# A fused attention, expert and GLU kernel: the second head's moves ahead of later loads, fills and RMS weights later, RMS in smaller steps

## The chip, the cores and the metric

The kernel runs on one core of a Trainium2 chip. Its time is the device time of one execution in microseconds (us). Before the change it took 735.92 us, the median of three runs (735.87 to 736.73). A profiled execution is one further run with the hardware profiler on; its rows are what the prediction is worked out from.

## The reference

Three layers follow each other. Attention has 2 batches of 8 heads (16 heads in all), 768 rows of 64 numbers each, in which a query sees only the keys of its own hash bucket; the bucket is six sign bits of a projection. Then each of the 1536 rows of 512 numbers goes to the one of eight experts that a gate picks. Last comes an RMS norm and a gated linear unit (GLU).

```python
q_bits = (np.einsum('bhsd,dk->bhsk', q, proj) > 0)          # and k_bits the same
mask = q_bucket[:, :, :, None] == k_bucket[:, :, None, :]
scores = np.where(mask, scale * np.matmul(q, k.transpose(0, 1, 3, 2)), -1000000000.0)
attn = np.exp(scores - scores.max(-1)); attn = attn / (attn.sum(-1) + 1e-09)
x = np.matmul(attn, v)                                       # -> 1536 rows of 512
expert_idx = np.argmax(x @ w_gate, axis=1)                   # E = 8, F = 1024
out[mask] = gate_w[mask, None] * (np.maximum(xe @ w1[e], 0.0) @ w2[e])
rms = np.sqrt(np.mean(x * x, axis=-1, keepdims=True) + 1e-06)
xn = x / rms * rms_g
g = xn @ w_gate; val = xn @ w_val                            # d_ff = 1536
out = (g * (1.0 / (1.0 + np.exp(-g))) * val) @ w_out
```

## The kernel before, in words

Every product is made of two parts: a number is split into a rounded part (hi) and the rest (lo), and TensorE (PE) multiplies hi by hi, hi by lo and lo by hi. The program is written by hand in the order in which each engine takes its instructions; each engine, and SP, which issues most DMAs, works through its own list in that order and waits where data are missing.

**Attention, about 14 to 262 us.** A head has six units of 128 queries; unit u is `divmod(u, 6)` of head and part (but for the last heads). In the loop over u a string of letters (ORDER) gives the steps: scores two units ahead (S, L563 and L564), maxima on VectorE (DVE; L568), exponentials on ScalarE (ACT; L582), transposes (T, L601), their split (L610, L611), products with v (A, L632 to L635). The last letter (f, fill_next) runs one piece of a generator from the list `fills` on PE, and the rest of that piece follows in the next unit (p, after_fill). Among these generators is `prep_head(n)`, which makes a head's operands:

- two transposes wf (L514) of the loaded k and q of the head (the tile kq); the cast kqh (ACT, L516) and the rest kql (DVE, L517). Of kqh and kql there is one buffer each (KQ = 1);
- `moves()` (L501 to L508): for each head but the first, six DMAs that SP issues and that copy halves of kqh and kql to other partitions, into qA, kB, qB, kA; head 0 has three of them and makes the rest with ACT and GpSimd (POOL);
- the projections wp (L544 to L546), the sign bits ft (DVE L551, POOL L552), and two DMAs of ft into qA and kA (L554, L555). The first scores of the head need all eight DMAs.

Where `moves()` stands is set by ML (L42): a head n < ML issues it behind the second cast (L520), any other head behind the first projection (L548). ML is 1, so this is head 0 alone. `load_head(n)` loads k and q, and for n > 1 also v; `split_v(n)` (L473) splits v on POOL into vst (L479, L480).

Ahead of the loop stand, in this order (L901 to L929): load_head(1), head 0's preparation, four pieces of head 1's (the transposes and casts), the loads of v of heads 0 and 1, of the expert gate's weights (wd), split_v(0), load_head(2), the load of the RMS weights rg, the scores of units 0 and 1, and four more pieces of head 1's preparation. `keep_warm` puts matmuls of no use between these. In the loop head n + 3 is loaded at the fourth unit of head n, and head n + 2 is prepared in head n.

The weights of the experts come in through `load_next` (L244), 512 KB each, from unit 6 on. `xs` is a buffer in DRAM, with a window of rows for each expert; before rows are scattered into it, `fill_windows(e)` (L159) writes 2 x 128 rows of an empty mark from the tile `fill`, two DMAs of 257 KB for each expert. Two experts come in each of the heads 1 to 4.

**Experts, about 264 to 442 us.** For each expert four steps f make the hidden part (ph, L1222 to L1224) and four its output (py, L1251 to L1253). Weights are split just in time (`convert`, ACT L284 and DVE L285), and the next weight's load is issued when a split has ended. `finish` takes the output rows of the expert before through `finish_rows` (L182): squares and a root, then on DVE the scaling by the RMS and rg (y, L205), and a scatter to `yd` in DRAM on POOL. It is a generator, and each of the steps f of the next expert takes one piece of it (L1231): the copies and squares, the root, and then the scaling and scattering of both halves of 128 rows in one. `load_y` brings rows of yd back as yt, and `flip_y` transposes them (f, L1141) for the GLU; the first flips stand in the last expert.

**GLU, about 442 to 727 us.** Matmuls of 512 columns, back to back; the last rows are scattered by POOL.

Of the kernel before, what the change touches and what calls it, by code (L numbers as in the profile page):

```python
# [19 lines left out]
P = 128  # L20
# [14 lines left out]
F0 = 3  # L35
XB = 4
P15 = 19
PTF = 2
U1 = 1
WARM = (20, 8, 8, 12, 24, 10, 4)  # L40
PT1 = 1
ML = 1  # L42


def turns(t):
# [28 lines left out]
def lsh_attention_moe_glu(  # L74
# [15 lines left out]
    nc = tc.nc  # L90
# [3 lines left out]
    E = moe_w_gate.shape[1]  # L94
    F1 = moe_w1.shape[2]
    F2 = moe2_w_gate.shape[1]
    T = S // P
# [56 lines left out]
    rg = const.tile([P, DM], F32, name="rg")  # L154
# [4 lines left out]
    def fill_windows(e):  # L159
        for j in range(W // P):  # L160
            nc.sync.dma_start(xs[e * N + j * P:e * N + (j + 1) * P, :], fill)
# [20 lines left out]
    def finish_rows(pool, ps_, gates, idents, places, tag, sort=False):  # L182

        J = len(ps_)
        y = pool.tile([P, J, DM + 1], F32, tag=f"y{J}", name=f"y{tag}")
        st = pool.tile([P, 8, J], F32, tag=f"yst{J}", name=f"yst{tag}")
        for j in range(J):
            if sort:
                nc.scalar.activation(halves(y[:, j, 0:DM]), sorted_(ps_[j]), AF.Copy, scale=gates[j])
            else:  # L190
                nc.scalar.activation(y[:, j, 0:DM], ps_[j], AF.Copy, scale=gates[j])
        for j in range(J):
            nc.scalar.activation(ps_[j], y[:, j, 0:DM], AF.Square, accum_out=st[:, 0, j:j + 1])
            nc.gpsimd.tensor_copy(y[:, j, DM:DM + 1], idents[j])
        yield
        nc.vector.tensor_scalar(st[:, 1], st[:, 0], 1.0 / DM, 1e-6, ALU.mult, ALU.add)
        nc.scalar.activation(st[:, 2], st[:, 1], AF.Sqrt)
        yield
        nc.vector.reciprocal(st[:, 3], st[:, 2])
        nc.vector.tensor_tensor(st[:, 4], st[:, 3], st[:, 3], ALU.mult)  # L200
        nc.vector.tensor_tensor(st[:, 4], st[:, 4], st[:, 1], ALU.mult)
        nc.vector.tensor_scalar(st[:, 5], st[:, 4], -0.5, 1.5, ALU.mult, ALU.add)
        nc.vector.tensor_tensor(st[:, 6], st[:, 5], st[:, 3], ALU.mult)
        for j in range(J):
            nc.vector.scalar_tensor_tensor(y[:, j, 0:DM], y[:, j, 0:DM], st[:, 6, j:j + 1], rg, ALU.mult, ALU.mult)  # L205
            ins = scatter("yd", yd, places[j], y[:, j], bounds_check=N - 1, oob_is_err=False)
            if tag in ends:
                tc.add_to_no_dep_group("ends", ins)
# [126 lines left out]
    with ExitStack() as ac:  # L335
# [5 lines left out]
        def load_head(n):  # L341
            if n >= NH:
                return
            b, h = divmod(n, H)
            kq = ld.tile([P, T, 2 * D], F32, tag="kq", name=f"kq{n}")
            for j in range(2 if n == 0 else 1):
                ts = slice(3 * j, 3 * j + 3) if n == 0 else slice(0, T)
                for i, src in enumerate((k, q)):
                    eng = nc.scalar if n == 0 and i == 1 else nc.sync
                    eng.dma_start(kq[:, ts, i * D:(i + 1) * D], src[b, h].rearrange("(p t) d -> p t d", t=T)[:, ts])  # L350
            if n == 0:
                for rs in (slice(0, D), slice(D, 2 * D)):
                    nc.sync.dma_start(pr[rs], proj)
            raw[n] = [kq]
            if n > 1:
                load_v(n)
# [22 lines left out]
        def keep_warm(count, pool, tag, **kw):  # L379

            if count:
                warms.append(1)
                t = pool.tile([P, 512], F32, tag=tag, name=f"warm{len(warms)}", **kw)
                for _ in range(count):
                    nc.tensor.matmul(t[:, 0:P], ones, ones, start=True, stop=True)
# [69 lines left out]
        done = []  # L455
# [27 lines left out]
        def prep_head(n, banks=("w",)):  # L483
# [57 lines left out]
            for j in range(2):  # L541
# [5 lines left out]
                yield  # L547
                if j == 0 and n >= ML:  # L548

# [363 lines left out]
            nc.sync.dma_start(wd[i * D:(i + 1) * D], moe_w_gate.rearrange("(h d) e -> d h e", d=D))  # L913
        split_v(0)
        cgen = constants()
        load_head(2)
        nc.sync.dma_start(rg, moe2_rms_g.partition_broadcast(P))

        scores(0)
        maxima(0)  # L920
# [5 lines left out]
        AH = 2  # L926
        for i in range(WARM[6]):
            next(fills[0])
        keep_warm(WARM[3], ps_w, "w")  # L929
        early = None  # L930
        for u in range(NU):
            n, t = divmod(u, T)
            g, i = divmod(u, 3)
            for step in ORDER if u < NU - LATE_N else LATE:
                if step == "m" and u + AH < NU:
                    maxima(u + AH)
                elif step == "n" and u + AH < NU:
                    shifts(u + AH)
                elif step == "o":
                    keep()  # L940
                elif step == "q":
                    after_give()
                elif step == "p":
                    after_fill()
                elif step == "r":
                    if slowly and next(slowly[0], 1) == 1:
                        slowly.pop()
                elif step == "v":
                    invert()
                elif step == "f":  # L950
                    fill_next()
                elif step == "F":
                    if u < NU - 1:
                        give()
                elif step == "T":
                    transposes(u)
                elif step == "H":
                    parts_of(2)
                elif step == "E" and u + 1 < NU:
                    exponentials(u + 1)  # L960
                elif step == "S" and u + 2 < NU:
                    scores(u + 2)
                elif step == "A" and g >= 1:
                    if g < 2 * NH - 2:
                        if i < len(AVS):
                            av(g - 1, AVS[i])
                    elif g == 2 * NH - 2:
                        if i == 0:
                            av(g - 1, range(T))
                    else:  # L970
                        if i < len(AVL):
                            av(g - 1, AVL[i])
                        if i > 0:
                            av(g, range(T), i - 1, 1)
            if u >= T and u % 2 == 0 and u < T + 2 * RAW:
                load_next()
            if t in (2, 5) and n > 0 and 2 * (n - 1) + t // 3 < E:
                fill_windows(2 * (n - 1) + t // 3)
            next(cgen, None)
            if t == VT:  # L980
                split_v(n + 1)
            if t == (PTF if n == 0 else PT0 if n + 2 < NH - 2 else PT1) and n + 2 < NH - 1:
                fills.insert(0, prep_head(n + 2))
            if u == NU - P15:
                fills.append(prep_head(NH - 1))
            if t == LT:
                load_head(n + 3)
            if t in SPL:
                if early is None and n >= 2 and at["piece"] < DEPTH - 1:
                    early = split_early()  # L990
                if early is not None and next(early, 1) == 1:
                    early = None
            if u >= NU - 7 and u < NU - 4:
                split_x(u - NU + 7)
            scatter_x()
            if u == NU - U1:
                while slowly:
                    if fills:
                        fill_next()
                        after_fill()  # L1000
                    if next(slowly[0], 1) == 1:
                        slowly.pop()
                while late:
                    scatter_x()
                start_first()
# [148 lines left out]
    with ExitStack() as mc:  # L1154
# [37 lines left out]
        def fill_pe():  # L1192
            while fillers and next(fillers[0], 1) == 1:
                fillers.pop(0)
# [14 lines left out]
        done = iter(())  # L1209
        flips = flip_y(0, NT)  # L1210
        for e in range(E):
# [30 lines left out]
            for f in range(NF):  # L1242
                i = e * 2 * NF + NF + f
                convert(i)
                wh, wl = part(i)[0:2]
                hh, hl = hid[f]
                for s_ in range(2):
                    fc = 2 * f + s_
                    for j in range(2):
                        js = slice(j * P, (j + 1) * P)  # L1250
                        nc.tensor.matmul(py[j], hh[:, s_, js], turns(wh[:, s_]), start=fc == 0, stop=False)  # L1251
                        nc.tensor.matmul(py[j], hh[:, s_, js], turns(wl[:, s_]), start=False, stop=False)  # L1252
                        nc.tensor.matmul(py[j], hl[:, s_, js], turns(wh[:, s_]), start=False, stop=fc == 2 * NF - 1)  # L1253
                parts.pop(i)
                fill_pe()
            done = finish(e, py)
        for _ in done:
# [110 lines left out]
```

## Time and profile before

| what | value |
|---|---|
| median of three runs | 735.92 us (735.87 to 736.73) |
| the profiled execution, its own time | 735.27 us |
| its span | 733.6 us |
| PE, DVE, ACT, POOL busy in the span | 717.4 (98%), 577.8 (79%), 402.9 (55%), 225.6 (31%) us |
| granted TensorE clock, mean | 0.998 |
| moved by the DMA queues | 103.44 MB, mean 141 GB/s |
| q1 (the DMAs of SP) | 76480 packets, 92.95 MB |

The span is what the profiler saw from the first to the last instruction; 1.7 us of the run lie around it. Times in rows count from the span's start. PE is busy nearly all the time, but matmuls are pipelined and their ends are modelled, so the gaps before single instructions, with what ended each, tell more than the busy share. PE's longest gaps behind the program's first microseconds are of 1.8 us (what follows them: scores, L563), 1.1 us (scores, L563), 0.9 us (f, L1141) and 0.7 us (wk, L753).

### The profile page before, as it was taken

The page shows a single profiled execution, that of the slowest core. Times are in us where ns is not written, and L with a number is a line of the kernel's source. Part 1 is how long each engine was busy: PE and PEld are TensorE (multiplying, and loading weights), DVE is VectorE, ACT ScalarE, POOL GpSimd, SP SyncE. Part 2 cuts the span into 40 slices and gives each one's busy share as a digit, 9 for nine tenths or more (in the row PEclk, how much of TensorE's full clock was granted, in tenths as well). Part 3 has the DMA queues.
Part 4 walks back from the last instruction along what each step waited for, and adds up shares of the span by engine and source line. Part 5 has one row for each costly group of instructions (what it writes and reads, how often), then busy time and mean ns, then how long its engine had stood idle before and what let it go on. Part 6 is the DMA issues. An engine that isn't in the chain of part 4 may idle for free.

```text
span 733.6 us, 12489 instructions
## 1 busy us (share of the span) xinstructions
PE 717.4 (98%) x4451; PEld 651.7 (89%) x4452; DVE 577.8 (79%) x1095; ACT 402.9 (55%) x805; POOL 225.6 (31%) x405
## 2 busy tenths in 40 slices
PE   8899999999999999999999999999999999999996
PEld 7798999999999889999999988888888888888885
DVE  6899999999999757787688777756777778778533
ACT  5798998998998735667665555533211222212210
POOL 5143344446635520213022313211211212211124
PEclk9999999999999999999999999999999999999999
DMA  7699856556742147677788674221221121200013
GB/s 182 163 254 263 213 152 154 139 147 173 190 109 70 45 146 246 197 222 246 249 264 265 218 250 150 97 87 58 61 84 58 57 87 59 86 29 1 0 58 115
DMA packets 80546, 103.44 MB, mean 141 GB/s; under 512 B 31799, under 2 KB 50231, under 8 KB 80480
## 3 DMA queue, kind: packets, MB, share of 16 engines
q1 hardware_dynamic: 76480, 92.95, 44.4%
q0 software_dynamic: 3200, 9.46, 3.5%
q8 instruction: 36, 0.59, 0.4%
q10 hardware_dynamic: 800, 0.20, 0.1%
q14 instruction: 30, 0.25, 0.1%
HBM read 69.53 MB, written 14.72 MB: 115 GB/s over the span
## 4 chain that ended last, share of the span: by engine, by line
PE 56%; issue 2%; POOL 2%; ACT 1%; DVE 1%; DMA 1%; SPq 0%; POOLq 0%; DVEq 0%
PE pg L1292 4%; PE pv L1293 4%; PE pg L1293 4%; PE pg L1291 4%; PE pv L1291 4%; PE pv L1292 4%; PE ph L1222 4%; PE ph L1223 4%; PE ph L1224 4%; PE py L1251 3%; PE py L1253 3%; PE py L1252 3%; PE z L1319 3%; PE z L1317 3%; PE z L1318 3%
## 5 line engine op out<-in xcount | busy, mean ns | idle before, releaser
L330 POOL TENSOR_TENSOR wa<-wa,hi 128x512 f32<-128x512 f32 x36 | 58.4, 1623 | 235.4 <-ACT hi L326 203.6
L326 ACT CAST hi<-wa 128x512 fp32r<-128x512 f32 x36 | 22.4, 621 | 151.3 <-DVE wa L324 147.2
L582 ACT ACTIVATE P<-S,negm 128x768 f32<-128x768 f32 x96 | 95.8, 998 | 10.5 <-DVE negm L573 6.4
L611 DVE TENSOR_TENSOR ptl<-T,pth 128x384 fp32r<-128x384 f32 x192 | 97.3, 547 | 1.5 <-ACT pth L610 0.8
L568 DVE TENSOR_REDUCE neg<-S 128x1 f32<-128x768 f32 x96 | 90.8, 946 | 3.6 <-PE S L564 2.9
L610 ACT CAST pth<-T 128x384 fp32r<-128x384 f32 x192 | 83.3, 488 | 3.6 <-PE T L601 2.9
L601 PE MATMUL T<-ident,P 128*128 128x128 f32 x576 | 81.8, 275 | 1.0 <-DVE ptl L611 0.5
L601 PEld LDWEIGHTS T<-ident,P 128*128 128x128 f32 x576 | 67.5, 141 | 7.8 <-DVE ptl L611 4.2
L285 DVE TENSOR_TENSOR lo<-raw,hi 128x1024 fp32r<-128x1024 f32 x58 | 68.7, 1216 | 4.6 <-ACT hi L284 4.6
L284 ACT CAST hi<-raw 128x1024 fp32r<-128x1024 f32 x58 | 60.2, 1055 | 21.0 <-DMA raw<-in_moe_w_dram 20.6
L563 PE MATMUL S<-kA,qA 76*128 76x384 f32 x192 | 66.2, 345 | 3.8 <-ACT kqh L516 1.8
L564 PE MATMUL S<-kB,qB 128*128 128x384 f32 x192 | 63.1, 329 | 0.4 <-DMA qB<-kql 0.4
L1222 PE MATMUL ph<-xTh,hi 128*128 128x256 f32 x224 | 62.6, 279 | 0.0
L1223 PE MATMUL ph<-xTl,hi 128*128 128x256 f32 x224 | 61.6, 275 | 0.0
L1224 PE MATMUL ph<-xTh,lo 128*128 128x256 f32 x224 | 61.6, 275 | 0.0
L633 PE MATMUL O<-ptl,vst 128*64 128x384 f32 (+1 forms) x198 | 59.8, 332 | 0.0
L1317 PE MATMUL z<-hi,hi 128*128 128x512 f32 x144 | 54.9, 381 | 0.0
L1291 PE MATMUL pg<-gxh,hi 128*128 128x512 f32 x144 | 54.7, 380 | 0.0
L1291 PE MATMUL pv<-gxh,hi 128*128 128x512 f32 x144 | 54.7, 380 | 0.0
L1292 PE MATMUL pg<-gxl,hi 128*128 128x512 f32 x144 | 54.7, 380 | 0.0
L1293 PE MATMUL pg<-gxh,lo 128*128 128x512 f32 x144 | 54.6, 379 | 0.0
L1292 PE MATMUL pv<-gxl,hi 128*128 128x512 f32 x144 | 54.6, 379 | 0.0
(236 smaller groups left out, 1911.8 us busy)
## 6 DMA issues: line engine op xcount, KB each, us to landing
raw<-in_moe_w_dram SPq DMA_DIRECT2D x64, 512.0 KB
raw<-in_moe_w_gate_dram SPq DMA_DIRECT2D x12, 512.0 KB
raw<-in_moe_w_val_dram SPq DMA_DIRECT2D x12, 512.0 KB
raw<-in_moe_w_out_dram SPq DMA_DIRECT2D x12, 512.0 KB
xs<-fill SPq DMA_DIRECT2D x16, 257.0 KB
xw<-xs SPq DMA_DIRECT2D x7, 514.0 KB
yt<-yd SPq DMA_DIRECT2D x12, 256.5 KB
qA<-kqh SPq DMA_DIRECT2D x16, 192.0 KB
```

What stands on the lines that cost most here:

```text
L568: nc.vector.tensor_reduce(neg[u % 4][:, 1:2], St[u][:, :, 0:HW], AX.XY, ALU.max, negate=True)
L582: nc.scalar.activation(p_, St.pop(u)[:, :, 0:HW], AF.Exp, bias=nm[:, 1:2], scale=nm[:, 0:1], accum_out=sums[n][:, t:t + 1])
L601: nc.tensor.transpose(w[:, c * P:(c + 1) * P], p_[:, j, c * P:(c + 1) * P], ident)
L610: nc.scalar.copy(hi[:, 3 * j:3 * j + 3, cs], wv)
L611: nc.vector.tensor_tensor(lo[:, 3 * j:3 * j + 3, cs], wv, hi[:, 3 * j:3 * j + 3, cs].bitcast(F32), ALU.subtract)
L1222: nc.tensor.matmul(ph[:, s_], wh[:, c, fs], turns(xh[:, c]), start=c == 0, stop=False)
L1223: nc.tensor.matmul(ph[:, s_], wh[:, c, fs], turns(xl[:, c]), start=False, stop=False)
L1224: nc.tensor.matmul(ph[:, s_], wl[:, c, fs], turns(xh[:, c]), start=False, stop=c == KC - 1)
L1291: nc.tensor.matmul(ps_, wh[:, c, fs], turns(xTh[b][:, c]), start=c == 0, stop=False)
L1292: nc.tensor.matmul(ps_, wh[:, c, fs], turns(xTl[b][:, c]), start=False, stop=False)
L1293: nc.tensor.matmul(ps_, wl[:, c, fs], turns(xTh[b][:, c]), start=False, stop=c == KC - 1)
L1317: nc.tensor.matmul(z, hi[:, s_, ts_], turns(oh_[:, s_]), start=s_ == 0, stop=False)
```

## The change

Four things change. ML goes from 1 to 2, so that head 1 issues its six moves behind its second cast, and load_head(2) goes behind the four later pieces of head 1's preparation. `fill_windows` runs in heads 6 to 9 instead of 1 to 4 (FN = 6). rg is loaded at unit 60, the first of head 10. `finish_rows` stops ahead of each half's scaling (a new yield), and the second four steps of an expert take pieces of it too.

```diff
-ML = 1
+FN = 6
+ML = 2
...
         for j in range(J):
+            yield
             nc.vector.scalar_tensor_tensor(y[:, j, 0:DM], y[:, j, 0:DM], st[:, 6, j:j + 1], rg, ALU.mult, ALU.mult)
...
         cgen = constants()
-        load_head(2)
-        nc.sync.dma_start(rg, moe2_rms_g.partition_broadcast(P))
...
             next(fills[0])
+        load_head(2)
         keep_warm(WARM[3], ps_w, "w")
...
-            if t in (2, 5) and n > 0 and 2 * (n - 1) + t // 3 < E:
-                fill_windows(2 * (n - 1) + t // 3)
+            if t in (2, 5) and 0 <= 2 * (n - FN) + t // 3 < E:
+                fill_windows(2 * (n - FN) + t // 3)
...
+            if u == 10 * T:
+                nc.sync.dma_start(rg, moe2_rms_g.partition_broadcast(P))
...
                 parts.pop(i)
+                next(done, None)
                 fill_pe()
```

PE and ACT keep their instructions in the same order. On SP, behind the third move of head 0 (qB_194), the order before is this (kqh_241 and kql_242 are head 1's, kq_274 and v_277 head 2's, v_265 and v_267 those of heads 0 and 1):

```order
L361 DMA v_265<-in_v_dram 128x384
L361 DMA v_267<-in_v_dram 128x384
L913 DMA wd<-in_moe_w_gate_dram 64x8x8 x2
L350 DMA kq_274<-in_k_dram 128x6x64
L350 DMA kq_274<-in_q_dram 128x6x64
L361 DMA v_277<-in_v_dram 128x384
L917 DMA rg<-in_moe_rms_g_dram 128x512
L508 DMA qA_306<-kqh_241 64x768
```

Five more moves follow it there, then the two DMAs of ft. Behind the same third move, the order of the changed kernel is this (ft_243 is head 1's; the numbers of the loaded tiles differ from before, v_275 and v_277 are heads 0 and 1, kq_317 is head 2):

```order
L510 DMA qA_259<-kqh_241 64x768
L510 DMA kB_256<-kql_242 64x768
L510 DMA qB_257<-kql_242 64x768
L510 DMA kA_258<-kqh_241 64x768
L510 DMA kB_256<-kqh_241 64x768
L510 DMA qB_257<-kqh_241 64x768
L363 DMA v_275<-in_v_dram 128x384
L363 DMA v_277<-in_v_dram 128x384
L915 DMA wd<-in_moe_w_gate_dram 64x8x8 x2
L556 DMA qA_259<-ft_243 12x768
L557 DMA kA_258<-ft_243 12x768
L352 DMA kq_317<-in_k_dram 128x6x64
```

The moves have gone ahead of the loads of v and wd, and head 2's loads have gone behind the two DMAs of ft. POOL's order there is the same in both kernels, and these rows of the changed one say what stands around head 1's ft:

```order
L541 TENSOR_SCALAR kA_195<-kA_195 12x384 x2
L481 TENSOR_SCALAR vst_281<-v_275 128x6x64
L482 TENSOR_TENSOR vst_281<-v_275,vst_281 128x6x64
L554 TENSOR_SCALAR ft_243<-ft_243 12x384 x2
L132 MEMSET fill 128x514
```

Nothing moved among them: the split of head 0's v stays ahead of ft. On DVE, in the last expert (index 7), the order before is this (y_6494 are the rows of expert 6, lo_6549 a weight's split, hl_6627 the hidden part's, gxl the flip's):

```order
L203 TENSOR_TENSOR yst_6495<-yst_6495 128x2
L205 SCALAR_TENSOR_TENSOR y_6494<-y_6494,yst_6495,rg 128x512 x2
L285 TENSOR_TENSOR lo_6549<-raw_6424,hi_6548 128x1024
L1229 SCALAR_TENSOR_TENSOR hl_6627<-ph_6601,hh_6626 128x512
L1147 TENSOR_TENSOR gxl_4625<-f_6630,gxh_4623 128x8x64
L1147 TENSOR_TENSOR gxl_4625<-f_6654,gxh_4623 128x8x64
```

And in the changed kernel, at the same place:

```order
L204 TENSOR_TENSOR yst_6495<-yst_6495 128x2
L287 TENSOR_TENSOR lo_6549<-raw_6424,hi_6548 128x1024
L1232 SCALAR_TENSOR_TENSOR hl_6617<-ph_6591,hh_6616 128x512
L207 SCALAR_TENSOR_TENSOR y_6494<-y_6494,yst_6495,rg 128x512
L1150 TENSOR_TENSOR gxl_4625<-f_6625,gxh_4623 128x8x64
L207 SCALAR_TENSOR_TENSOR y_6494<-y_6494,yst_6495,rg 128x512
L1150 TENSOR_TENSOR gxl_4625<-f_6654,gxh_4623 128x8x64
```

The two y have gone behind the weight's split and the hidden part's, and stand one by one.

## Rows read from the trace of the kernel before

**Rows 1.** Stages: span, busy us of engines, clock, DMA share, GB/s.

```profile
60.00:80.00 20.00, 18.94 (x137) 17.67 (x137) 18.80 (x38) 17.01 (x38) 8.52 (x20) 1.00 0.95 246
100.00:150.00 50.00, 50.00 (x366) 46.95 (x365) 49.03 (x106) 45.68 (x102) 20.50 (x47) 1.00 0.58 147
```

**Rows 2.** Timeline of PE: start, us, instruction, idle before it and its releaser.

```profile
22.13 0.49 PE L514 MATMUL wf<-evens,kq 128*128 128x128 f32 x3
24.43 0.40 PE L563 MATMUL S<-kA,qA 76*128 76x384 f32 x1 [1.81 <-ACT kqh L516]
26.86 0.49 PE L514 MATMUL wf<-evens,kq 128*128 128x128 f32 x3
27.11 0.41 PE L563 MATMUL S<-kA,qA 76*128 76x384 f32 x1
...
70.73 0.40 PE L563 MATMUL S<-kA,qA 76*128 76x384 f32 x1 [1.06 <-DMA kA<-ft]
...
439.32 0.63 PE L1141 MATMUL f<-ident,yt 128*128 128x128 f32 x4 [0.86 <-DMA yt<-yd]
```

**Rows 3.** Timeline of SP's queue of DMAs, start of the program.

```profile
6.02 0.54 SPq L508 DMA_DIRECT2D qA<-kqh  x1
...
7.24 0.59 SPq L508 DMA_DIRECT2D qB<-kql  x1
7.89 1.12 SPq L361 DMA_DIRECT2D v<-in_v_dram  x2
...
17.16 0.67 SPq L508 DMA_DIRECT2D qB<-kqh  x1
...
18.94 0.75 SPq L555 DMA_DIRECT2D kA<-ft  x1
...
20.46 0.64 SPq L350 DMA_DIRECT2D kq<-in_q_dram  x1
```

**Rows 4.** Timeline of ACT, the cast of head 2.

```profile
23.72 0.58 ACT L516 ACTIVATE kqh<-wf,scv 128x384 fp32r<-128x384 f32 x1 [1.54 <-DMA qB<-kqh]
```

**Rows 5.** Timeline of DVE and POOL, head 1's preparation.

```profile
10.56 1.14 DVE L517 SCALAR_TENSOR_TENSOR kql<-wf,scv,kqh 128x384 fp32r<-128x384 f32 x2 [1.29 <-DMA qB<-kql]
...
11.02 0.52 POOL L479 TENSOR_SCALAR vst<-v 128x384 fp32r<-128x384 f32 x1 [2.17 <-DMA v<-in_v_dram]
11.62 1.02 POOL L480 TENSOR_TENSOR vst<-v,vst 128x384 fp32r<-128x384 f32 x1
14.43 1.08 POOL L552 TENSOR_SCALAR ft<-ft 12x384 fp32r<-12x384 f32 x2 [1.79 <-DVE ft L551]
```

**Rows 6.** Timeline, ACT's first loads of q and who waits for them.

```profile
0.84 1.06 ACTq L350 DMA_DIRECT2D kq<-in_q_dram  x2
...
4.47 0.50 PEld L514 LDWEIGHTS wf<-evens,kq 128*128 128x128 f32 x3 [0.19 <-DMA kq<-in_q_dram]
```

**Rows 7.** Timeline: head 4's kA<-ft on SP, first maxima of heads on DVE.

```profile
65.10 0.77 SPq L555 DMA_DIRECT2D kA<-ft  x1
...
25.43 0.96 DVE L568 TENSOR_REDUCE neg<-S 128x1 f32<-128x768 f32 x1 [0.48 <-PE S L564]
...
55.97 0.95 DVE L568 TENSOR_REDUCE neg<-S 128x1 f32<-128x768 f32 x1
...
87.04 0.94 DVE L568 TENSOR_REDUCE neg<-S 128x1 f32<-128x768 f32 x1
...
101.96 0.94 DVE L568 TENSOR_REDUCE neg<-S 128x1 f32<-128x768 f32 x1
```

**Rows 8.** Timeline of DVE and SP, the last expert.

```profile
429.88 1.42 DVE L205 SCALAR_TENSOR_TENSOR y<-y,yst,rg 128x512 f32<-128x512 f32 x2
...
433.05 3.22 SPq L1130 DMA_DIRECT2D yt<-yd  x3
```

**Rows 9.** Stages of PE alone at the program's end.

```profile
728.00:730.00 2.00, 0.00 (x0) 1.00 0.46 174
730.00:732.00 2.00, 0.00 (x0) 0.51 0.23 88
```

## The prediction

> **What bounds the kernel now.** I read the page's busy shares first, then the stages, then every idle gap of PE, and last the queues behind the three large gaps. PE is busy for 98% of the span, so the stages have to say what paces it. In the attention's quiet stretch PE shows no idle time, but DVE is busy 49.03 of 50 us; between 60 and 80 us both lose about one microsecond, and there the DMA share is 0.95 against 0.58 later [rows 1]. The reader is to see that attention is paced by DVE and PE together, with nothing to catch up a delay with, and that the other stages are PE's own. So a gap of PE that shows in DVE too goes into the end time, one for one. The gaps that the change can reach are three [rows 2]: 1.81 us before the scores at 24.43 (the first ones of head 1), 1.06 us before the scores at 70.73 (head 4), 0.86 us before the transposes at 439.32 (the flip of the rows of yd). They make 3.7 us, 0.5% of the span: that is the most the change could bring, if it put nothing in their place.
>
> **Part 1, the order at the start: a loss.** Before, the two loads of v, the loads of wd, kq and v of head 2 and rg stand ahead of head 1's six moves. The stall at 24.43 is the end of that queue: the last of the six moves is issued at 17.16 and head 2's cast on ACT, which overwrites its source, gets going only at 23.72, 1.54 us late; kA<-ft, the last piece that the scores need, is issued behind it at 18.94 [rows 3, 4]. The change puts the moves first, so that these transfers are early. What is late next is v of head 0. POOL keeps its order, and there the two operations on v (vst, L479 and L480) stand ahead of the two that finish ft of head 1 (L552) [rows 5]. kA<-ft waits for these, and the loads of kq for head 2, which stood ahead of it in SP's queue, now stand behind it. PE takes wf of head 2 (22.13) before the scores of head 1. So everything on PE now hangs on one chain: moves, v, vst, ft, kA<-ft, kq, wf.
>
> Step by step. kB<-kql of head 1 cannot be issued before DVE's two kql are done, at 10.56 + 1.14 = 11.70 [rows 5]; nothing in front of that moves, since head 0's three moves keep their places. Five moves of about 0.62 us of issue each (0.59 for qB<-kql, 0.67 for the last) put v at 11.75 + 3.1 = 14.85, where it was issued at 7.89 [rows 3]. When v has landed: before, it was the fourth of a stream that began at 6.02 and POOL had it at 11.02, 5.0 us later [rows 3, 5]; now it is the sixth of one that begins at 11.75, and each further move of 197 KB takes 0.8 us at the 246 GB/s of the busy stretch [rows 1]: 11.75 + 5.0 + 1.6 = 18.35. The floor is v's own 3.1 us from issue to use, 14.85 + 3.13 = 17.98. The ceiling is what the last move took in before's crowded queue, 23.72 - 17.16 = 6.56, so 21.4 [rows 3, 4]. I take 18.8, near the stream's figure, a little late because v itself must pass too.
> - POOL: vst 1.62 us from the start of L479 to the end of L480, ft 1.08 [rows 5]: ft is done at 21.5.
> - SP: from the start of kA<-ft to the end of the second load of kq behind it, 20.46 + 0.64 - 18.94 = 2.16 [rows 3]: issued by 23.7.
> - kq lands 4.47 - 1.90 = 2.57 us after the end of its issue where the queues are empty, as at the program's start [rows 6]: 26.3.
> - PE: wf at 26.3 instead of 22.13, the scores 0.25 behind it (26.86 to 27.11) [rows 2]: 26.55 instead of 24.43, 2.1 us later.
> - DVE: the cast of head 2 on ACT and its kql on DVE follow wf, at about 26.9 and 27.5, where the cast began at 23.72 [rows 4]: 3.2 us later, of which DVE wins back some, since it stood idle behind the old stall too.
> I take a loss of 2.4 us, between PE's figure and DVE's; with v at its floor it is 1.3 by PE's figure, with v at its ceiling 2.4 + 2.6 = 5.0.
>
> **Part 2, fills and rg later: a gain.** At head 4 kA<-ft is issued at 65.10 and its data are waited for until 70.73 [rows 2, 7]: the queue is full (60 to 80 us, share 0.95). Of sixteen fills of 257 KB, the eight of heads 1 and 2 are issued ahead of it, 2.1 MB or 8.6 us of transfer at 246 GB/s [rows 1]. They move to heads 6 to 9; the backlog goes. The worth is read from the pace: from head 3's first maxima to head 5's DVE takes 87.04 - 55.97 = 31.07 us, while the next head takes 101.96 - 87.04 = 14.92 [rows 7]; 31.07 - 2 x 14.92 = 1.23. The lower bound is 0 (something else late), and PE's own gap, 1.06, stands between; I take 1.2. Where the fills go, the traffic rises from 147 GB/s by 4.2 MB in four heads of 14.9 us, 71 GB/s, to 218, under the 246 of the full stretch: I cost it at nothing, hidden beside DVE. rg is one more load of 256 KB in head 10, read first in the experts: nothing.
>
> **Part 3, the smaller steps of RMS: a gain.** In the last expert, DVE's two y (1.42 us from 429.88) stand ahead of a split (lo, L285), that split's end ahead of a load on SP, and the load ahead of yt, issued at 433.05 [rows 8]. The fourth flip waits for this yt, 0.86 us [rows 2]. With the y behind lo, the split begins where they began, and yt can be issued up to 1.42 us earlier, which covers 0.86. Bounds: 0, if the landing is set by the transfers ahead and not by the issue, and 0.86; I take 0.8. In the other experts the same y moves by a step, beside PE's work; PE has no other wait there, and the later load of xw is used only two experts on: nothing.
>
> **The sum.** +2.4 - 1.2 - 0.8 = +0.4 us. The profiled run took 735.27 us (span 733.6), 0.65 below the median of 735.92, so +0.4 gives 735.7 on its scale and 736.3 on the median's. About 0.2%, 1.5 us, is what a measurement of this kernel can tell from no change: below 734.4 is faster, above 737.4 slower. I forecast no change that can be told: 0.48.
>
> **The rivals.**
> - Slower through a longer stall. It has two forms of one mechanism, a PE that stands still too long at 22.1. PE's idle time grows from 1.81 to about 4 us. The page's clock row shows no fall at the 1.81; at the program's end it was still 1.00 in 728 to 730, all idle, and 0.51 in 730 to 732, that is, it fell to 1.2 GHz after a pause of some length between these [rows 9]. If it falls here, the work behind the wait runs at half the pace; PE has no slack there, and if the next 4 us pass so, half of their work, 2.0 us by that estimate, is late. With +0.4 that is +2.4, 738.3. The other form: v lands over a microsecond later than I take it, as things did in before's crowded queue, which alone gives +1.5 or more and makes the pause longer. It decides from v at 19.9. For it: one chain with no slack. Against: the moves run into an empty queue. 0.35.
> The Trainium skill, page "TensorE: Matmul & The Clock Gate", section "HAM oscillation — how this bites in real kernels", says that a wait of TensorE for a transfer, once long enough, throttles its clock, and that the work behind the wait then starts cold. By that rule the reordering makes exactly such a wait, and the time would be the 738.3 above; the trace agrees for the end of the program, and no row shows it for a wait between.
> - Faster. The first stall ends at v's floor (+1.3), part 2 gives its 1.23 and, with the crowding gone, the refill after the first stall shrinks too: head 1's and head 2's maxima run from 25.43 to 55.97 [rows 7], 30.54 against 29.84, 0.7 us. Then 1.3 - 1.23 - 0.86 - 0.7 = -1.5, 734.4. For it: all three gaps are real and the change aims at each. Against: it needs everything at its end, and v cannot be issued earlier than 14.85. 0.17, which also holds a chain that I have wrong in some link.
> - The fills only change place: a gap of the kind of 70.73 at one or more of heads 7 to 10. Against: 218 GB/s is under what the queues moved. Price 1.2 each, which for one of them gives 737.5; it is in the 0.35 above.
>
> The range: 734.6 holds most of the faster case, 738.9 the longer stall with the clock; the likeliest case alone, no clock loss, v between 18.0 and 19.9, is 735.2 to 737.4.
>
> **What would show it.** Right: in the profile after, POOL's first vst starts near 18.8 and ft ends near 21.5; a PE gap of about 4 us ends in wf of head 2, released by the DMA of kq, near 26.3; the scores of head 1 follow at once and no longer wait for kqh or kA; no gap near 70; the flip near 439 does not wait; fills around 105 to 165 us without a gap. Wrong: vst starting before 18 (SP's queue is not in order as I read it) or after 20; a granted clock below 1.00 between 22 and 32 us (the first rival); a gap at head 4 as before; new gaps between 105 and 165 us; or a yt wait that stays.

## The result and the profile after

The change makes the kernel slower. It took 741.87 us (median of 6 runs, 740.78 to 742.57) where the kernel before took 735.89 beside it (6 runs, 734.74 to 736.73): a ratio of 1.0082 with a 95% interval of 1.0066 to 1.0097, some 6.0 us. The forecast was 736.3 in a range of 734.6 to 738.9, so the time lies outside. The profiled execution took 741.72 us with a span of 740.0, against 735.27 and 733.6.

The chain that the prediction named is there. POOL shows its middle: v of head 0 is waited for, then cut, and only then ft of head 1 is finished (start, us, instruction, idle before it and its releaser).

```profile
19.72 0.52 POOL L481 TENSOR_SCALAR vst<-v 128x384 fp32r<-128x384 f32 x1 [11.08 <-DMA v<-in_v_dram]
20.32 1.00 POOL L482 TENSOR_TENSOR vst<-v,vst 128x384 fp32r<-128x384 f32 x1
21.41 1.09 POOL L554 TENSOR_SCALAR ft<-ft 12x384 fp32r<-12x384 f32 x2
```

SP's queue on both sides of it, same columns:

```profile
14.41 0.61 SPq L510 DMA_DIRECT2D qB<-kqh  x1
15.06 1.09 SPq L363 DMA_DIRECT2D v<-in_v_dram  x2
...
22.52 0.78 SPq L557 DMA_DIRECT2D kA<-ft  x1
...
24.07 0.64 SPq L352 DMA_DIRECT2D kq<-in_q_dram  x1
```

The moves end at 15.0 and not at 17.8 [rows 3], as intended. But kA<-ft is issued 3.6 us later than before, and head 2's kq is issued behind it. On PE this comes out as one gap, and slow work behind it:

```profile
28.05 0.88 PE L516 MATMUL wf<-evens,kq 128*128 128x128 f32 x3 [5.43 <-DMA kq<-in_q_dram]
28.57 0.67 PE L565 MATMUL S<-kA,qA 76*128 76x384 f32 x1
29.04 0.53 PE L566 MATMUL S<-kB,qB 128*128 128x384 f32 x1
...
33.20 0.59 PE L516 MATMUL wf<-evens,kq 128*128 128x128 f32 x3
```

The three stages that answer to [rows 1] (columns as there: the clock is the last but two):

```profile
25.00:30.00 5.00, 1.95 (x8) 1.89 (x9) 0.42 (x1) 1.04 (x2) 0.36 (x2) 0.66 0.91 231
30.00:35.00 5.00, 5.00 (x27) 4.71 (x26) 3.12 (x9) 3.03 (x7) 0.33 (x2) 0.66 0.00 1
60.00:80.00 20.00, 20.00 (x147) 18.80 (x145) 19.69 (x42) 18.52 (x43) 7.79 (x20) 1.00 0.59 146
```

After the gap the granted clock is 0.66 in the mean of these stretches: PE runs at 1.2 GHz for a part of them, its matmuls of 384 columns take 0.53 and not 0.33 us. From the scores to the next wf it needs 33.20 - 28.57 = 4.63 us, where it needed 26.86 - 24.43 = 2.43 [rows 2]. Between 60 and 80 us PE has no gap any more and the DMA share fell from 0.95 to 0.59, as intended by part 2.

The last expert, the fourth and the last flip on PE (the first of the two waited for yt before [rows 2]):

```profile
444.44 0.60 PE L1144 MATMUL f<-ident,yt 128*128 128x128 f32 x4
...
457.81 0.66 PE L1144 MATMUL f<-ident,yt 128*128 128x128 f32 x4 [1.09 <-DVE gxl L1150]
```

DVE's first maxima of heads 3 and 5, which tell how far attention has come:

```profile
62.35 0.95 DVE L570 TENSOR_REDUCE neg<-S 128x1 f32<-128x768 f32 x1
...
92.34 0.94 DVE L570 TENSOR_REDUCE neg<-S 128x1 f32<-128x768 f32 x1
```

Followed through the two profiled executions, PE (or DVE, which goes with it) stands behind the kernel before by:

| place | before | after | behind by |
|---|---|---|---|
| first scores of head 1 | 24.43 | 28.57 | 4.14 |
| next wf of head 2 | 26.86 | 33.20 | 6.34 |
| first maxima of head 3 (DVE) | 55.97 | 62.35 | 6.38 |
| first maxima of head 5 (DVE) | 87.04 | 92.34 | 5.30 |
| first ph of the experts | 264.74 | 270.62 | 5.88 |
| fourth flip | 439.32 | 444.44 | 5.12 |
| last flip | 451.64 | 457.81 | 6.17 |
| span | 733.6 | 740.0 | 6.4 |

So: +4.1 by the chain, +2.2 by the clock behind it, -1.1 at head 4, +0.6 at the change to the experts, and at the flips a gain that is taken back.

### The profile page after: what moved, and what is told of

The parts are those of the page before. It is cut to its first block, busy times and chain, and to the rows that moved or that the text cites. A ratio compares the mean times of both kernels' runs of the same rounds, so it can differ in the third digit from the quotient of the medians.

```text
span 740.0 us, 12487 instructions
## 1 busy us (share of the span) xinstructions
PE 720.1 (97%) x4451; PEld 653.9 (88%) x4452; DVE 578.9 (78%) x1095; ACT 403.0 (54%) x805; POOL 236.9 (32%) x405
## 4 chain that ended last, share of the span: by engine, by line
PE 56%; issue 2%; POOL 2%; DVE 2%; ACT 1%; DMA 0%; POOLq 0%; DVEq 0%
PE ph L1225 4%; PE ph L1226 4%; PE ph L1227 4%; PE pv L1297 4%; PE pv L1296 4%; PE pv L1295 4%; PE pg L1296 4%; PE pg L1297 4%; PE pg L1295 4%; PE py L1254 4%; PE py L1255 4%; PE py L1256 3%; PE z L1322 3%; PE z L1323 3%; PE z L1321 3%
## 5 line engine op out<-in xcount | busy, mean ns | idle before, releaser
L169 POOL DMA_INDIRECT yd<-y,posw x16 | 36.0, 2251 | 105.7 <-ACT hi L286 68.1
```

## The experiments

The theory: part 1 carries the whole loss, by one chain (moves, v, vst, ft, kA<-ft, kq, wf) and by the clock that falls behind the wait; part 2 gives its microsecond; part 3 gives nothing, because another chain stands right behind the one it shortens. The rivals: the fills and the RMS steps carry part of the loss; having the moves first is itself the fault; the slow clock is hidden beside DVE.

The experiments ran in three series, each on one chip. There the kernel before took 738 to 740 us in the median and scattered (735.0 to 743.9); every ratio is to its runs in the same series.

**Part 1 alone.** `ML = 2` and `load_head(2)` behind the four pieces; everything else as before.

> The kernel before with part 1 alone: head 1's moves first, head 2's kq and v loaded behind the four pieces of head 1's preparation; fills, rg and RMS as before. Theory A (the start carries the whole loss: one chain of moves, v, vst, ft, kA<-ft, kq, wf makes a PE wait of about 5.4 us, the granted clock falls behind it, and the two together move attention by the +6.4 us that the changed kernel shows at head 2's first maxima): ratio about 1.0085, +6 to +6.5 us, a wait of over 5 us ahead of wf, and PE at 1.2 GHz behind it. With fills and rg still in the stretch between, the gap at head 4 is seen again, so the time is at or above that of the changed kernel. Theory B (the loss comes from the moved fills or from the RMS steps, the start costs the +2.4 of the prediction): ratio about 1.0033.

Ratio 1.0077 (1.0049 to 1.0105), median 746.37. PE waits 5.11 us for kq ahead of wf at 28.08, and the clock is 0.82 and 0.84 in the two stages from 25 to 35 us. The gap at head 4, expected again, is only 0.40 us here (at 75.74). Part 1 alone makes a loss of this size; its seven runs scatter from 742.21, the profiled one, to 748.28.

**Part 2 alone.** The fills under `n - FN`, rg at unit 60.

> The kernel before with part 2 alone: the fills of the windows begin at head 6 and rg is loaded in head 10. Theory A: the gap of 1.06 us ahead of head 4's scores goes and no other comes between 100 and 170 us: ratio about 0.9986, -1.0 us (-1.2 by the prediction). Theory B (the fills only change place): a gap of about 1 us at one of the heads 7 to 10, ratio 1.000 or more.

Ratio 0.9947 (0.9927 to 0.9967), median 736.50 against 739.66: 3 us faster, more than either theory had. Two rows of PE and one stage say why, and what stays.

```profile
23.36 0.40 PE L564 MATMUL S<-kA,qA 76*128 76x384 f32 x1 [0.60 <-DMA qA<-ft]
...
439.43 0.63 PE L1143 MATMUL f<-ident,yt 128*128 128x128 f32 x4 [1.95 <-DMA yt<-yd]
```

```profile
439.00:443.00 4.00, 3.57 (x13) 3.01 (x14) 3.18 (x7) 1.10 (x3) 1.58 (x1) 0.69 0.97 304
```

The gap at head 4 is gone, as expected. The wait at the start has shrunk to a third as well, though no fill is issued that early in the kernel before: the reader is to suspect rg. And behind the wait for yt, 1.95 us, the clock is 0.69.

**Part 3 alone.** The new `yield` and the new `next(done, None)`.

> The kernel before with part 3 alone: the RMS of the finish is taken in smaller steps. Theory A (the wait for yt at the last flip goes, but DVE's own chain of y and gxl at the end of the last expert is the hidden bound, so the wait comes back at the flip for gxl, and a flip of expert 5 waits too): no change or a small loss, ratio 1.000 to 1.0006. Theory B (the prediction's: the 0.86 us of the wait are gained): ratio 0.9989, -0.8 us.

Ratio 0.9991 (0.9968 to 1.0014): no change that can be told, no gain of 0.8 us seen. The fourth flip doesn't wait, but the first one waits 1.29 us for yt and the last one 1.18 for gxl. Its start showed something else, in the scores of head 1 on PE and the stage behind them:

```profile
24.85 0.40 PE L564 MATMUL S<-kA,qA 76*128 76x384 f32 x1 [2.06 <-ACT kqh L517]
```

```profile
25.00:30.00 5.00, 5.00 (x24) 4.63 (x25) 2.63 (x8) 2.81 (x7) 0.32 (x2) 0.66 0.03 9
```

Part 3 touches nothing there. The kernel before stands at an edge: this wait was 1.81 us with the clock at 1.00 behind it [rows 2], and here 2.06 with the clock at 0.66.

**PE kept busy through a part of its wait.** The changed kernel, and in the loop at unit 3:

```diff
             for step in ORDER if u < NU - LATE_N else LATE:
+                if u == 3 and step == "f":
+                    keep_warm(60, ps_w, "w")
```

> The changed kernel with 60 extra small bf16 matmuls on ones on PE, whose result nobody reads, right ahead of wf of head 2, so that PE works through most of its wait of 5.4 us. Nothing else moves. Theory A (the clock's fall behind the wait costs time of its own): the granted clock stays at 1.00 from 25 to 35 us, the matmuls between the first scores of head 1 and the next wf take 0.33 us and not 0.53, wf ends its wait at 28.05 as before this edit, and the time is 1.5 to 2.2 us under the changed kernel's: about 739.9, ratio to the kernel before 1.0055. Theory B (DVE is late anyway, and the slow matmuls lie beside its work): the clock stays up and the time is within 0.5 us of the changed kernel's 741.9, ratio 1.0075 to 1.0085.

Ratio 1.0042 (1.0022 to 1.0062), and the changed kernel itself was not run in this series. It settled nothing: the 60 matmuls took 3.52 us, an idle rest of 2.24 remained ahead of wf at 28.35, and the clock was 0.82 from 25 to 30. So it was made again with more of them, beside the changed kernel.

**The kernel before, and the changed one, once more.**

> The kernel before itself, for a profile on this chip, on which its times scatter from 736.6 to 743.9 us. Theory A (it stands at the edge: a start wait of 1.8 us leaves the granted clock at 1.00, one of 2.1 us, as in the run with part 3 alone, lets it fall, and in many executions it falls): a profiled time of 739 or more shows a start wait of 2 us or more, or a wait for yt of about 1.9 us, with a clock below 1.00 behind it. Theory B (the scatter is spread thinly over the transfers): waits as in the first profile, 1.81 and 0.86 us, and no clock below 1.00 before the end.

One profiled execution, 742.46 us: a start wait of 2.22 us for kqh with a clock of 0.66 from 25 to 30 us, and a wait for yt of 2.82 with 0.87 and 0.70 in the two stages of 4 us from 443 to 451. The first theory holds for this execution: the kernel before lost its clock in it, at two places. In how many others it does is not shown. Nor is the clock all of the 7.2 us over the first profile: 2.2 of them arise between the first ph of the experts and the first flip, where it stays at 1.00.

> The changed kernel itself, on the same chip as the next two. Theory A: the wait ahead of wf of head 2 is again 5 us or more and the clock falls behind it; the difference to the kernel before is smaller than on the first chip where the kernel before loses its clock too: ratio 1.004 to 1.007. Theory B (the loss does not depend on the state of the kernel before): 1.0082.

Ratio 1.0061 (1.0038 to 1.0085), median 742.66 against 738.09. PE waits 4.7 us for kq, the clock is 0.63 and 0.69 in the two stages. The expected 1.004 to 1.007; 1.0082 lies inside the interval as well.

**PE kept busy through the whole wait.** As above with 90.

> The changed kernel with 90 instead of 60 extra small matmuls ahead of wf of head 2, about 5.3 us of work, so that the idle rest of the wait is under 0.8 us. With 60 a rest of 2.24 us was left and the clock fell again behind it. Theory A: the clock stays at 1.00 from 25 to 35 us, the matmuls behind the wait take 0.33 us, and attention is 2 us earlier from head 2 on: ratio to the changed kernel of the same call 0.9975, -1.5 to -2.2 us. Theory B (DVE's work hides the slow matmuls): within 0.5 us of the changed kernel of the same call.

Median 741.01, 1.65 us under the changed kernel of the same series (ratio 1.0037, 1.0021 to 1.0052). PE's rows:

```profile
22.87 5.20 PE L387 MATMUL warm<-ones 128*128 128x128 bf16 x90
27.90 0.50 PE L516 MATMUL wf<-evens,kq 128*128 128x128 f32 x3
28.19 0.40 PE L565 MATMUL S<-kA,qA 76*128 76x384 f32 x1
...
30.56 0.49 PE L516 MATMUL wf<-evens,kq 128*128 128x128 f32 x3
```

```profile
25.00:30.00 5.00, 5.00 (x71) 4.95 (x69) 0.95 (x2) 1.56 (x4) 0.01 (x1) 1.00 0.88 227
```

wf starts as late as in the changed kernel (27.62 in the same series), so the chain is the same. But from the scores to the next wf it is 2.37 us, not 4.63 as in both profiles of the changed kernel. Head 3's first maxima on DVE come at 59.66 and not at 61.99. The clock's price in the changed kernel is these 2.2 us, and DVE does not hide them. Ten of the twelve runs lie under all six of the changed kernel.

**Two orders put back.** The changed kernel; the moves stay first, but head 2's loads stand ahead of the four pieces again, and `split_v(0)` behind them.

```diff
-        split_v(0)
         cgen = constants()
+        load_head(2)
...
             next(fills[0])
-        load_head(2)
+        split_v(0)
```

> The changed kernel, with head 1's moves still first, but head 2's kq and v loaded ahead of the four pieces of head 1's preparation as in the kernel before, and head 0's v cut on POOL behind these pieces instead of ahead of them. Theory A (the loss is the chain v, vst, ft, kA<-ft, kq, wf, not the moves' place): the wait ahead of wf falls below 1 us, the scores of head 1 start by 24.4 us at the latest, the clock stays at 1.00, and with part 2's gain the time is about 1 to 2 us under the kernel before: ratio 0.997 to 0.9985. Theory B (with the moves first, v lands too late for anything behind it, whatever the order on POOL): a wait of 3 us or more at the values' matmuls or at wf, ratio 1.004 or more.

Ratio 0.9999 (0.9977 to 1.0020): the loss is gone, the hoped gain is not there. Two shorter waits stand on PE in place of the one, with one wf between them:

```profile
23.43 0.52 PE L516 MATMUL wf<-evens,kq 128*128 128x128 f32 x3 [1.00 <-DMA kq<-in_q_dram]
25.31 0.40 PE L565 MATMUL S<-kA,qA 76*128 76x384 f32 x1 [1.37 <-DMA kA<-ft]
```

The clock is 0.66 from 25 to 30 us here too. The expectation that the scores start by 24.4 failed: kA<-ft now waits in SP's queue behind head 2's loads, issued at 22.56.

**rg alone.** The kernel before, with rg loaded at unit 60.

> The kernel before with one edit: the load of rg, one DMA of 256 KB, is issued in head 10 and not ahead of head 1's six moves. The run with all of part 2 showed the first scores of head 1 at 23.36 with a wait of 0.60, where the kernel before has 24.43 to 24.99 with waits of 1.81 to 2.22. Theory A (rg alone did that: its transfer stood ahead of the moves): the scores of head 1 start by 23.6, the wait there is under 1 us, the clock stays at 1.00 from 25 to 30 us, the gap at head 4 stays, and the ratio is about 0.9965 on this chip, where the kernel before often loses its clock. Theory B (the fills did it, or chance): the wait is 1.8 us or more as before, ratio 1.000.

Ratio 0.9985 (0.9967 to 1.0003). At the start the first theory holds in full: the scores of head 1 start at 22.46 with no wait. The gain is lost at head 4:

```profile
69.60 0.40 PE L563 MATMUL S<-kA,qA 76*128 76x384 f32 x1 [1.97 <-DMA kA<-ft]
```

```profile
70.00:74.00 4.00, 4.00 (x18) 3.57 (x18) 2.27 (x5) 1.12 (x3) 0.00 (x0) 0.57 1.05 252
```

There the fills of heads 1 and 2 hold up kA<-ft as before, PE has come earlier and waits 1.97 and not 1.06 us [rows 2], and the clock falls behind it. So the move of rg needs the move of the fills; the fills without rg were not tried.

**Parts 2 and 3.**

> Parts 2 and 3 without part 1. Theory A (part 1 carries the loss, part 2 the whole gain, part 3 nothing or a little through the shorter wait for yt): ratio 0.994 to 0.996, as with part 2 alone (0.9947); the start wait is 0.6 us, the wait for yt at the fourth flip is gone and one for gxl of about 1.1 us is there in its place. Theory B (part 3 gains its 0.8 us once the start is out of the way): 0.9935 or less, at least 0.8 us under part 2 alone of the same call.

Ratio 0.9944 (0.9921 to 0.9966). That is part 2 alone, within the interval; part 2 alone was not run in this series. What part 3 does is seen on PE at the first and at the last flip, and in SP's waits between 405 and 440 us (in total, times, longest):

```profile
430.58 0.63 PE L1144 MATMUL f<-ident,yt 128*128 128x128 f32 x4 [1.76 <-DMA yt<-yd]
...
453.12 0.66 PE L1144 MATMUL f<-ident,yt 128*128 128x128 f32 x4 [1.14 <-DVE gxl L1150]
```

```profile
SPq L1133 <- DMA yd<-y,posw: 7.0, 1, 7.0
```

The kernel before has no such wait of SP in that stretch. Expert 5's second scatter is a step later, and the first load of yt waits 7.0 us for it at the head of SP's queue.

**Part 2, and PE kept busy ahead of the fourth flip.** 16 matmuls on ones in `flip_y`, at the tile that waits.

```diff
+            if tt == first + YB:
+                for _ in range(16):
+                    nc.tensor.matmul(w[:, 0], ones, ones, start=True, stop=True)
```

> Part 2 alone, and 16 extra small matmuls on ones on PE (about 0.95 us of work, results overwritten) right ahead of the transposes of the fourth flip, where the run with part 2 alone waited 1.95 us for yt and then ran at a clock of 0.69 for the next 4 us. Theory A (that wait costs more through the clock than by itself): the idle rest is about 1.0 us, the clock stays at 1.00 from 439 to 447, the matmuls py behind it stay at 0.38 us, and the time is 1.0 to 1.7 us under part 2 alone: ratio 0.9925 to 0.9935. Theory B (DVE's chain of y and gxl sets the end of the last expert anyway): a wait for gxl takes its place, ratio 0.9945.

Ratio 0.9946 (0.9923 to 0.9969), the lowest median, 734.40, but not to be told from the two others. The idle rest is 1.12 us and the clock 1.00 in all four stages from 432 to 448; the gain over part 2 alone is not shown.

**v cut late.** The changed kernel with one line moved.

```diff
-        split_v(0)
         cgen = constants()
...
         load_head(2)
+        split_v(0)
```

> The changed kernel with one edit: head 0's v is cut on POOL behind head 1's last two pieces and head 2's loads, so that ft no longer waits for v; head 2's kq is still loaded behind kA<-ft. Theory A (the link from v to ft holds up kq): ft is done 1.5 us or more earlier than 22.5, kq of head 2 is issued by 22.5 and landed by 26, the wait ahead of wf is 2.5 to 3.5 us, still long enough for the clock to fall, and the time is 1.5 to 2.5 us under the changed kernel's 742.7 of this chip: ratio 1.002 to 1.004. Theory B (the issue of the moves and kA<-ft hold it up and v hardly does): the wait stays above 4.5 us and the ratio at 1.006.

Ratio 0.9986 (0.9969 to 1.0004), where the changed kernel had 1.0061 in the series before, on another chip: better than expected. POOL's ft and v, then PE's wf and the stage behind it:

```profile
14.41 1.08 POOL L554 TENSOR_SCALAR ft<-ft 12x384 fp32r<-12x384 f32 x2 [5.61 <-DVE ft L553]
20.18 0.52 POOL L481 TENSOR_SCALAR vst<-v 128x384 fp32r<-128x384 f32 x1 [4.69 <-DMA v<-in_v_dram]
```

```profile
24.57 0.52 PE L516 MATMUL wf<-evens,kq 128*128 128x128 f32 x3 [1.51 <-DMA kq<-in_q_dram]
```

```profile
25.00:30.00 5.00, 5.00 (x39) 4.69 (x39) 4.26 (x11) 4.87 (x12) 0.32 (x2) 1.00 0.38 93
```

v lands no earlier, but ft is done 7 us sooner, kA<-ft and kq follow, the wait is 1.51 and not 5.43 us, and the clock holds. That link, ft behind v on POOL, made the loss against the kernel before. (The profiled execution is the slowest of the twelve, 740.88 us: at the first flip PE waits 2.24 us for yt in it, with a clock of 0.62 behind that.)

What is left of part 1 is not free even so. Parts 2 and 3 without part 1 took 734.92 us in this same series, and this kernel 738.11. Its attention is 2.0 us behind theirs at head 3 already, as DVE's first maxima show, theirs first:

```profile
54.34 0.95 DVE L570 TENSOR_REDUCE neg<-S 128x1 f32<-128x768 f32 x1
```

```profile
56.33 0.94 DVE L570 TENSOR_REDUCE neg<-S 128x1 f32<-128x768 f32 x1
```

Here PE still waits 0.68 us for vst and then the 1.51 for kq, and it has neither wait with parts 2 and 3 alone. That the moves at the head of the queue do no harm is therefore not shown.

## Why the prediction was wrong

- **The bound, the chain and its place: right.** Part 1 puts everything on one chain, and late v moves PE's wf; undoing the one link takes the loss against the kernel before away. PE's delay stays in the program one for one, as said: 6.34 us at head 2's wf, 6.38 at head 3's maxima. Of the signs of being wrong one came, the clock below 1.00 between 22 and 32 us.
- **The sizes in the chain: too small.** "I take 18.8" for v: it was 19.72, 0.9 later. "kq lands 2.57 us after the end of its issue": 28.05 - (24.07 + 0.64) = 3.34, 0.8 more. The 2.57 was read from half a load: the x2 of [rows 6] are the two halves of head 0's q, 98 KB each by the code. Head 2's kq comes in whole loads of 197 KB, the second behind kA<-ft and the first, and with v cut late it was the same again, 24.57 - (20.59 + 0.64) = 3.34. How much of the 0.8 is the size and how much the queue isn't shown. The scores came 0.52 behind wf and not 0.25, since the clock was already down. Together 2.0: 28.57 in place of 26.55. The term of 2.4 was 4.1 by PE's figure.
- **The clock: this step failed.** The forecast let PE stand still for about 4 us and counted nothing for what follows, because no fall was seen at 1.81 us and rows 9 showed one only at the program's end; the loss stood in the first rival, at 0.35. That rival priced it at 2.0, the trace shows 2.2. And it took its two forms, the clock and a late v, one for the other, where the longer wait brings both. Put together from the prediction's own prices (+0.4 + 2.0 + 1.5) they give 739.8; the range should have reached there, though that is still 2 us under the measured time. The Trainium skill, page "TensorE: Matmul & The Clock Gate", section "HAM oscillation — how this bites in real kernels", spoke against the forecast: after a wait for a transfer the next work starts cold. The trace agrees, with 0.66 behind the 5.43 us, and with 1.00 where the same wait was filled with work.
- **Part 2: right at head 4, -1.1 for -1.2, no new gap; wrong on rg.** "rg is one more load ... nothing" missed that it stands ahead of head 1's moves in the kernel before. Taken out alone, it ends the stall of 1.81 us there. In the change this gain cannot be seen, since the moves go first anyway: part 1 and the move of rg aim at the same stall, and part 1 makes a longer one.
- **Part 3: the wait went, the gain did not come.** The fourth flip does gain 0.99 us (from 6.11 behind at the first flip, 435.32 against 429.21, to 5.12). But DVE and ACT don't follow. DVE's chain of splitting weights paces there. It goes on from the third flip, ahead of the wait that went (441.41 against 435.27, 6.14 behind); its last y stands 455.74 - 449.57 = 6.17 behind, gxl behind it, and PE waits 1.09 us for that. And "in the other experts ... nothing" was wrong: with expert 5's scatter a step later, SP's first load of yt waits 6.3 us in the changed kernel. Part 3 moves waits rather than ending them. In seven of the eight profiles with part 3 PE waits for yt at the first flip, 0.44 to 2.24 us (in the result's own it does not), and in all eight for gxl at the last. In the six without part 3 it does neither, and waits at the fourth flip instead. DVE's last y before and after:

```profile
449.57 1.42 DVE L205 SCALAR_TENSOR_TENSOR y<-y,yst,rg 128x512 f32<-128x512 f32 x2
```

```profile
455.74 1.42 DVE L207 SCALAR_TENSOR_TENSOR y<-y,yst,rg 128x512 f32<-128x512 f32 x2
```

- **Not foreseen:** 0.6 us where the experts begin, 0.5 of it a longer wait of PE's sequencer (0.85 for 0.36). Other kernels of this study show 0.3 to 0.9 there, with and without part 1; what decides it stays open.

The sum: 4.1 + 2.2 - 1.1 + 0.6 + 0.3 for the last expert, and 0.3 in small shifts, give the 6.4 of the spans. The forecast had +0.4. Of the 6.0 between them the clock makes 2.2, the chain's size 1.7, part 3 1.1 (+0.3 in place of -0.8), the start of the experts 0.6, the rest small shifts.

Part 2 without part 1 beats both kernels: 0.9944 to 0.9947 of the time of the kernel before in three variants, some 4 us. On the chips of the experiments a part of this may be the clock, which the kernel before lost in the one execution that was profiled there; how much remains where that clock holds, as in the first profile, wasn't tried.

## What to carry to other kernels

When a DMA queue's order is changed, follow each engine's program order as well: a late transfer holds up what stands behind its consumer on that engine, here ft behind v, though the two have nothing to do with each other. A forecast that lets PE stand still for longer than any wait of the trace has to price the slow clock behind it as the likely case. And of a wait that is to go, ask first which other engine's chain ends right behind it.

## What the runs showed of the hardware

The clock fell behind idle waits of PE of 1.95 to 2.82 us at four places (the start with 2.06 and 2.22, head 4 with 1.97, yt with 1.95, 2.24 and 2.82, wf with 2.24); it held at 1.00 behind waits of 1.51, 1.73, 1.76 and 1.81, and also behind one of 2.02 and one of 2.13. It fell behind the three waits of 4.68, 5.11 and 5.43 us too, and behind two waits of 1.00 and 1.37 us that had only one wf between them. So the length of one wait does not by itself tell whether the clock falls, and a kernel whose longest wait lies near these may run with the fall or without: two profiled executions of the kernel before took 735.27 and 742.46 us, the second with the clock down at two places.
